# Two score tiles instead of one during the first batch, first query tails by SP's queue, and separate first-batch priorities, in a list-scheduled attention and mixing kernel

## The chip, the cores and the metric

One core of a Trainium2 chip runs the whole program. The metric is the device time of one execution in microseconds (us); the median of three timed executions before the change is 1014.8 us (1014.17 to 1015.2). The profile comes from one further execution.

## What is computed

The shapes are batch 8, 8 heads, sequence 576, head size 64, model size 512, all fp32. Each batch goes through attention in which scores below the row maximum less `tau` are dropped, and then through a token and channel mixing block. Cut to what matters:

```python
scores = scale * np.matmul(q, k.transpose(0, 1, 3, 2))
thresh = np.max(scores, axis=-1, keepdims=True) - tau
scores = np.where(scores >= thresh, scores, -1000000000.0)
attn = np.exp(scores - np.max(scores, axis=-1, keepdims=True))
attn = attn / (np.sum(attn, axis=-1, keepdims=True) + 1e-09)
x = heads_merged(np.matmul(attn, v))
theta = x @ w_theta
y = einsum('ts,bsd->btd', w_tok_r, x * cos(theta)) + einsum('ts,bsd->btd', w_tok_i, x * sin(theta))
u = x + y
out = u + np.maximum(u @ w_ch, 0.0)
```

## The kernel before

**The work.** The eight heads of a batch are four pairs, and each pair has nine score halves of 128 query rows by 576 keys (two heads by four blocks, and one half that holds the 64 last queries of both heads, the "tails"). For a half, TensorE (PE) writes the scores into a tile `s_ps` of two PSUM banks (line 633); VectorE (DVE) copies them out as `sc` and keeps the row minimum (648); ScalarE (ACT) adds the offset (660) and takes the exponential (669); DVE masks and sums (677, `s_sb`); PE transposes the result in four or five 128x128 pieces into one-bank tiles `t_ps` (717, 753); ACT copies those out (728, 730, 757, 761). When the nine halves of a pair are there, forty matmuls make its output `o_ps` in two banks (801).

Four pairs make a batch, and then its mixing runs (`mixture`): angles `m_ps` (939), sines on ACT, transposes `z_ps` (1053), the token product `y_ps` (1103), and the channel product (939 again). The mixing of one batch runs beside the attention of the next.

**The weights.** `w_theta`, `w_tok` and `w_ch` come in as wider numbers. During the first batch, each of nine token chunks and four `w_theta` chunks is loaded as `wraw`, goes through ACT (334, the absolute value `mag`), five DVE instructions (338, 342, 347, 352, 356), ACT (361, the high part), PE (385, 386, into `w_ps`) and ACT (389, the low part).

**The order.** Nothing is scheduled by the compiler. `Plan` collects every piece of work with its engine, an assumed duration, what it needs, a rank, and the slots it takes from named pots. `Plan.run` then walks an assumed clock: at each step it takes the engine that can start soonest and, among that engine's works that could start within a small slack, the one of the lowest rank; the instructions are written out in that order. Ranks come from the table `LEAD`. On the chip each engine runs its list in order and waits on semaphores.

PSUM has eight banks: the pot `pair` has one slot (two banks, for `s_ps`), the pot `bank` has six (one bank each, for `t_ps`, `w_ps`, `o_ps`, `r_ps`, `m_ps`, `y_ps`, `z_ps`). While the plan's clock is under 190 us, the slot `bank5` is kept for dummy matmuls `fill_ps` (line 274): 14 at the start, and some in every gap on PE that the plan sees above 0.5 us.

For pair 0 the two tail pieces of the queries are loaded by ACT's DMA queue (line 287) ahead of everything else on ACT; all other loads are SP's.

Of the kernel before, what the change touches and what calls it, by code (L numbers as in the profile page):

```python
# [10 lines left out]
F32 = mybir.dt.float32  # L11
# [18 lines left out]
STEP = 3.2  # L30
# [6 lines left out]
FILL = 0.2165  # L37
FILL_GAP = 0.5
# [48 lines left out]
class Plan:  # L87
# [9 lines left out]
    def run(self):  # L97
# [7 lines left out]
        filling = True  # L105
        if self.filler:
            pot, slot, fill = self.filler
            pot.free[slot] = NEVER
            fill(14)
        wait = {e: [w for w in self.works if w.eng == e and not w.left] for e in engines}  # L110
        todo = len(self.works)
        while todo:
# [22 lines left out]
            if self.filler and filling and w.eng == "PE":  # L135
                gap = at - free["PE"]
                if free["PE"] > FILL_UNTIL:
                    filling = False
                    pot.free[slot] = at
                elif free["PE"] > 0.0 and gap > FILL_GAP:  # L140
                    fill(int((gap - 0.2) / FILL))
# [24 lines left out]
def tile_attn_moe(  # L166
# [26 lines left out]

    plan = Plan()
    pots = {}
# [4 lines left out]
    for name, n in (  # L200
# [17 lines left out]
    def lead(name):  # L218
        return LEAD[name] * STEP
# [14 lines left out]
    FIRST = 4.9  # L234
# [33 lines left out]
    spare = []  # L268

    def fill(n):  # L270
        if not spare:
            spare.append(psum.tile([P, 512], F32, tag="bank5", name="fill_ps", bufs=1))
        for _ in range(n):
            nc.tensor.matmul(spare[0], dummy[:, :P], dummy, start=True, stop=True)  # L274

    plan.filler = (pots["bank"], 5, fill)
# [177 lines left out]
    def at(t):  # L454
        return t * STEP

    def first_parts(pr, qr, kr, dq, dk, rank):
# [23 lines left out]
        t = on_act(0.2, tail_high, [plan.add("ACT", 0.0, int, (), -99.0, FIRST - HOP)], rank, (pr.tails,))  # L481
# [8 lines left out]
    def prepare(n):  # L490

        pr = pairs[n] = SimpleNamespace(n=n, b=n // NP, p=n % NP, st=[], values=[], normal=[], a={}, scores=[[], []])
        rank = at(NU * n) + lead("prep")
# [99 lines left out]
    def attention(h):  # L593
# [176 lines left out]
        if k == NU - 1:  # L770
            values(pr, at(h) + lead("values"))
# [475 lines left out]
```

## Time and profile before

| | |
|---|---|
| median of three timed runs | 1014.8 us |
| profiled execution | 1013.25 us, its span 1011.4 us |
| PE busy | 999.1 us, 99% |
| DVE busy | 774.2 us, 77% |
| ACT busy | 647.1 us, 64% |
| GpSimd (POOL) busy | 234.4 us, 23% |
| granted TensorE clock, mean | 0.997 |
| dummy matmuls | 73, busy 24.1 us |

Busy times of PE count an instruction until its modelled end, so that two matmuls that follow each other overlap in them; the distance between two starts tells what one costs. A share over the whole span hides stages: the first 115 us, in which the first batch's attention and the weights run without any mixing, and the rest have different limits.

### The profile page before, as it was taken

What the parts mean: (1) busy time and instruction counts of PE and PEld (TensorE: products, weight loads), DVE (VectorE), ACT (ScalarE), POOL (GpSimd) and SP (SyncE); (2) the same over time, 40 slices, a digit from 0 to 9 for tenths busy, and PEclk for the clock granted to TensorE, in tenths of its full rate; (3) what the DMA queues carried; (4) which work ended last, traced back from release to release, by engine and by line L of the source; (5) the groups of instructions that cost most, each with busy time, mean ns of one, the idle gap of its engine ahead of it and who ended that gap; (6) DMA issues with size and microseconds to landing.
All of it is one profiled execution on the core that took longest, in us unless ns stands there. A gap on an engine that the chain in (4) does not pass through costs nothing.

```text
span 1011.4 us, 20944 instructions
## 1 busy us (share of the span) xinstructions
PE 999.1 (99%) x7597; PEld 896.5 (89%) x7597; DVE 774.2 (77%) x2038; ACT 647.1 (64%) x1292; POOL 234.4 (23%) x162
## 2 busy tenths in 40 slices
PE   7999999999999999999999999999999999999998
PEld 5777789889999999999999989899999999999898
DVE  5999788877987688766987679776888679876563
ACT  4888888645776468654785467764686448854430
POOL 1111123032342114311341123421143113400100
PEclk8999999999999999999999999999999999999999
DMA  6568756657654575337744475445763377441502
GB/s 198 157 191 239 212 147 183 163 166 228 170 128 119 140 215 155 98 96 203 198 126 117 98 227 174 108 119 156 217 160 82 90 204 214 112 101 34 172 22 68
DMA packets 86950, 151.89 MB, mean 150 GB/s; under 512 B 27200, under 2 KB 36672, under 8 KB 86848
## 3 DMA queue, kind: packets, MB, share of 16 engines
q1 hardware_dynamic: 86544, 150.53, 53.8%
q8 instruction: 60, 0.98, 0.4%
q14 instruction: 42, 0.34, 0.1%
q10 hardware_dynamic: 304, 0.03, 0.0%
HBM read 81.89 MB, written 13.78 MB: 95 GB/s over the span
## 4 chain that ended last, share of the span: by engine, by line
PE 95%; DVE 3%; DMA 1%; issue 0%; ACT 0%; POOL 0%; ACTq 0%; POOLq 0%
PE y_ps L1103 23%; PE m_ps L939 20%; PE s_ps L633 16%; PE o_ps L801 16%; PE t_ps L717 12%; PE z_ps L1053 3%; PE t_ps L753 2%; PE w_ps L385 2%; PE fill_ps L274 1%; DMA tail_raw<-in_qT_dram 1%; DVE sc L648 1%; DVE s_sb L677 1%; PE w_ps L386 0%; PE r_ps L832 0%; DVE bits L347 0%
## 5 line engine op out<-in xcount | busy, mean ns | idle before, releaser
L648 DVE TENSOR_SCALAR_CACHE_REDUCE sc<-s_ps,small 128x576 f32<-128x576 f32 x288 | 234.0, 812 | 59.6 <-PE s_ps L633 57.6
L677 DVE SCALAR_TENSOR_TENSOR s_sb<-sc,nm,s_sb 128x576 f32<-128x576 f32 x288 | 237.8, 838 | 23.9 <-ACT s_sb L669 23.1
L669 ACT ACTIVATE s_sb<-sc,nm 128x576 f32<-128x576 f32 x288 | 221.8, 783 | 25.1 <-DVE sc L648 24.8
L728 ACT COPY a<-t_ps 128x512 f32<-128x512 f32 x256 | 148.2, 589 | 100.0 <-PE t_ps L717 99.4
L633 PE MATMUL s_ps<-kd,qq 128*128 128x288 f32 x992 | 181.0, 304 | 0.6 <-DVE sc L648 0.3
L717 PE MATMUL t_ps<-ident,s_sb 128*128 128x128 f32 x1152 | 170.4, 273 | 0.0
L1103 PE MATMUL y_ps<-wt_l,zh 128*128 128x288 f32 x576 | 167.1, 304 | 0.0
L1103 PE MATMUL y_ps<-wt_h,zh 128*128 128x288 f32 x576 | 166.4, 307 | 0.0
L801 PE MATMUL o_ps<-a,v 128*64 128x256 f32 (+1 forms) x1280 | 162.3, 408 | 0.0
L633 PEld LDWEIGHTS s_ps<-kd,qq 128*128 128x128 f32 x992 | 143.6, 189 | 8.0 <-DVE sc L648 5.8
L801 PEld LDWEIGHTS o_ps<-a,v 128*64 128x64 f32 x1280 | 89.1, 137 | 63.9 <-issue 5.3
L717 PEld LDWEIGHTS t_ps<-ident,s_sb 128*128 128x128 f32 x1152 | 137.2, 140 | 6.6 <-issue 5.3
L297 POOL TENSOR_TENSOR khl<-kraw,khl 128x576 fp32r<-128x576 f32 x31 | 48.4, 1562 | 357.2 <-ACT khl L529 195.0
L1103 PEld LDWEIGHTS y_ps<-wt_l,zh 128*128 128x128 f32 x576 | 108.4, 189 | 0.2
L1103 PEld LDWEIGHTS y_ps<-wt_h,zh 128*128 128x128 f32 x576 | 108.0, 189 | 0.5
L1103 PE MATMUL y_ps<-wt_h,zl 128*128 128x288 f32 x576 | 107.2, 298 | 0.0
L1034 POOL TENSOR_TENSOR z<-z,xT 128x576 f32<-128x576 f32 x56 | 80.2, 1465 | 85.6 <-ACT z L1019 85.6
L939 PE MATMUL m_ps<-xh,wm 128*128 128x288 f32 x512 | 94.0, 303 | 0.0
L939 PE MATMUL m_ps<-uh,wm 128*128 128x288 f32 x512 | 92.1, 303 | 0.6 <-DVE xT L1157 0.6
L812 ACT COPY xT<-o_ps 128x320 f32<-128x320 f32 x64 | 25.6, 400 | 100.7 <-PE o_ps L801 100.7
L1103 PEld LDWEIGHTS y_ps<-wt_h,zl 128*128 128x128 f32 x576 | 85.7, 188 | 0.0
L939 PEld LDWEIGHTS m_ps<-uh,wm 128*128 128x128 f32 x512 | 74.4, 189 | 3.4 <-issue 2.3
(98 smaller groups left out, 1433.2 us busy)
## 6 DMA issues: line engine op xcount, KB each, us to landing
wm<-wm_dram SPq DMA_DIRECT2D x64, 512.0 KB
kd<-khl SPq DMA_DIRECT2D x62, 288.0 KB
qq<-qhl SPq DMA_DIRECT2D x124, 128.0 KB
kd<-khl SPq DMA_DIRECT2D x62, 256.0 KB
v<-in_vp_dram SPq DMA_DIRECT2D x32, 320.0 KB
kraw<-in_kT_dram SPq DMA_DIRECT2D x32, 288.0 KB
qraw<-in_qT_dram SPq DMA_DIRECT2D x32, 288.0 KB
rb<-rows_dram SPq DMA_DIRECT2D x64, 144.0 KB
```

Source lines behind the costliest of these rows:

```text
L297: eng.tensor_tensor(out=out, in0=a, in1=b, op=ALU.subtract)
L633: nc.tensor.matmul(ps.tile[:, half, to], st, kk[:, fr], start=(x == 0), stop=(x == len(terms) - 1))
L648: nc.vector.tensor_scalar(out=sc.tile.rearrange("p (a b) -> p a b", a=2), in0=ps.tile[:, :, :HS], scalar1=gate, scalar2=None, op0=ALU.mult ...
L669: nc.scalar.activation(out=u.s.tile[:, j], in_=sc.tile, func=AF.Exp, bias=nm.tile[:, 0:1], scale=-1.0)
L677: nc.vector.scalar_tensor_tensor(out=e, in0=sc.tile, scalar=nm.tile[:, 1:2], in1=e, op0=ALU.is_le, op1=ALU.mult, accum_out=pr.rows.tile[:, ...
L717: nc.tensor.transpose(out=bank.tile[:, c * P : (c + 1) * P], in_=sf[:, k0 + c * P : k0 + (c + 1) * P], identity=ident)
L728: nc.scalar.copy(out=t.a[:, :, j, q0 : q0 + P], in_=bank.tile.rearrange("p (c q) -> p c q", c=4))
L801: nc.tensor.matmul(bank.tile[64 * j : 64 * j + 64, :w], st, mv, start=(c == 0), stop=(c == 4))
L939: nc.tensor.matmul(banks[h].tile[:, :HS], wm.tile[:, a, c, :], x[:, h * HS : (h + 1) * HS], start=(key == 0), stop=(key == 11),)
L1034: eng.tensor_tensor(out=zi, in0=zi, in1=xs[m].x.tile, op=ALU.mult)
L1053: nc.tensor.transpose(out=bank.tile[:, i * P : (i + 1) * P], in_=z.tile[:, c : c + P], identity=ident)
L1103: nc.tensor.matmul(bank.tile[:, :HS], st, (wt_l if wl else wt_h)[:, c, hs], start=(k + q == 0), stop=(k + q == 26),)
```

## The change

The PSUM pool is split. A second slot of the pot `pair` and the slots `bank4` and `bank5` share the same two banks in time. At first a pool `psum0` holds the second `pair` slot, so scores have two tiles of two banks, and the other tiles have four banks. When the plan's clock has passed `split` (114.84) and that slot is free, the pool is closed, a pool `psum1` is opened in its place, the `pair` slot is taken out for good, and the two new `bank` slots come in: one pair and six banks from then on, as before.

The dummy matmuls lose their own bank: they take any `bank` slot that is free early enough, 12 or more of them before the first real matmul (how many follows from the plan), and then in gaps above 0.4 us where a slot is free.

The two tail pieces of pair 0's queries are loaded by SP, behind the first `kraw`, and their copy on ACT gets a rank of its own place in the plan. Most entries of `LEAD` get a second value that is added in the first batch only; the weights' ranks change (`wt`, `wt_step`, and new `wk`, `wk_step`). The first token product no longer waits for all token chunks. The assumed duration of the score copy goes from 0.68 to 0.74, with its `pair` slot free 0.08 before the plan's end of it. No computing instruction is added or removed but the dummies.

```diff
-FILL = 0.2165
-FILL_GAP = 0.5
+FILL = 0.228
+FILL_GAP = 0.4
...
-    wt=1.24, wt_step=-3.72, wch=0.63, wch_step=-5.29, wlow=10.19, xh=-17.5, xlast=15.0, angle=1.82, ztok=1.52,
+    wt=0.48, wt_step=-10.83, wch=-3.05, wch_step=-0.24, wlow=14.42, xh=-17.5, xlast=15.0, angle=1.82, ztok=1.52,
...
-    cev=-16.07, dma=1.13, hop=0.13,
+    cev=-16.07, dma=1.13, hop=0.13, split=114.84, wk=-17.47, wk_step=-2.88, score0=-31.88, empty0=-6.42,
+    offset0=15.77, power0=16.19, mask0=-7.4, flip0=-2.74, evict0=-0.54, flip50=-11.41, values0=-13.64,
+    vevict0=-110.27, norm0=-7.09, prep0=-17.86, vload0=10.11, inv0=21.92, times0=17.78, mix0=-2.15, span0=0.08,
...
-        filling = True
-        if self.filler:
-            pot, slot, fill = self.filler
-            pot.free[slot] = NEVER
-            fill(14)
+        filled = False
+        pair, bank = self.pots["pair"], self.pots["bank"]
+        bank.free[4] = bank.free[5] = NEVER
+        split = False
...
+            if not split and at > LEAD["split"] and pair.free[1] < NEVER:
+                split = True
+                bank.free[4] = bank.free[5] = max(at, pair.free[1])
+                pair.free[1] = NEVER
+                self.resplit()
+            if w.eng == "PE" and free["PE"] < FILL_UNTIL:
                 gap = at - free["PE"]
...
+                slot = min(range(4), key=lambda k: bank.free[k])
+                if not filled:
+                    filled = True
+                    self.filler(12 + max(0, int((at - 6.7) / FILL)), slot)
+                elif gap > FILL_GAP and bank.free[slot] < free["PE"] - 0.5:
+                    self.filler(int((gap - 0.2) / FILL), slot)
+                    bank.free[slot] = at
...
-        ("pair", 1), ("bank", 6), ("raw", 3), ("wm", 3), ("z", 3), ("xh", 4), ("xl", 4), ("zh4", 4), ("zl4", 4),
+        ("pair", 2), ("bank", 6), ("raw", 3), ("wm", 3), ("z", 3), ("xh", 4), ("xl", 4), ("zh4", 4), ("zl4", 4),
...
+        if (tag, h.slot) in (("pair", 1), ("bank", 4), ("bank", 5)):
+            p = extra[-1]
...
-    for j in range(2):
-        r = slice(64 * j, 64 * j + 64)
-        nc.scalar.dma_start(tail_raw[r, r], qT[0, 0, j, :, 512:])
...
-        t = on_act(0.2, tail_high, [plan.add("ACT", 0.0, int, (), -99.0, FIRST - HOP)], rank, (pr.tails,))
+        def load_tail(r):
+            return lambda: nc.sync.dma_start(tail_raw[r, r], qT[0, 0, r.start // 64, :, 512:])
+
+        loads = []
+        for j in range(2):
+            w = on_sp(load_tail(slice(64 * j, 64 * j + 64)), loads[-1:] and [issued(loads[-1])], rank - 0.05, (), 16)
+            w.ready = 1.45
+            loads.append(w)
+        t = on_act(0.2, tail_high, loads, rank, (pr.tails,))
...
-        d1 = on_dve(0.68, empty, [s], at(h) + lead("empty"), (sc, nm), 0.08)
-        ps.until(d1)
+        d1 = on_dve(0.74, empty, [s], at(h) + lead("empty", n // NP), (sc, nm), 0.08)
+        ps.until((d1, -0.08))
...
-                    if b == 0 and m == 0:
-                        need += [w for r in wt_ready for w in r]
```

How the order moves is seen in three places. The first is the start of ACT's list. `tails` is the copy of the tail pieces, `mag` the first step of a weight chunk, `part` the high half of the first keys or queries. Before:

```order
L258 DMA small<-in_tau_dram 128x1
L287 DMA tail_raw<-in_qT_dram 64x64 x2
L288 ACT_TABLE_LOAD
L476 CAST tails<-tail_raw 128x128
L334 ACTIVATE mag<-wraw 128x576 x2
L361 ACTIVATE wt_h<-bits 128x576
L464 CAST part<-kraw 128x576
L464 CAST part<-qraw 128x576
```

Now:

```order
L275 DMA small<-in_tau_dram 128x1
L302 ACT_TABLE_LOAD
L348 ACTIVATE mag<-wraw 128x576 x2
L375 ACTIVATE wt_h<-bits 128x576
L478 CAST part<-kraw 128x576
L490 CAST tails<-tail_raw 128x128
L478 CAST part<-qraw 128x576
```

The two tail loads have left ACT's queue, and the copy of the tails stands behind two steps of weights and the keys' high half instead of at the head.

The second place is SP's list at the start, with the loads of the first weight chunks, keys, queries and values. Before:

```order
L329 DMA wraw<-in_w_tok_dram 128x1152 x2
L507 DMA kraw<-in_kT_dram 128x576
L507 DMA qraw<-in_qT_dram 128x576
L516 DMA v<-in_vp_dram 128x640
L507 DMA kraw<-in_kT_dram 128x576
```

Now:

```order
L343 DMA wraw<-in_w_tok_dram 128x1152 x2
L529 DMA kraw<-in_kT_dram 128x576
L496 DMA tail_raw<-in_qT_dram 64x64 x2
L529 DMA qraw<-in_qT_dram 128x576
L529 DMA kraw<-in_kT_dram 128x576
```

The tail loads stand behind the first keys and ahead of the first queries; the weight chunks keep the head.

The third place is PE's list in pair 0, from the second chunk's last sum on. A half's scores are six matmuls of 288 columns, or nine in three widths. Before:

```order
L386 MATMUL w_ps<-wt_h,minus 128x288
L633 MATMUL s_ps<-part 128x64 x3
L633 MATMUL s_ps<-part 128x224 x3
L633 MATMUL s_ps<-part 128x288 x3
L717 MATMUL t_ps<-ident,s_sb 128x128 x4
L274 MATMUL fill_ps<-dummy 128x512 x2
L717 MATMUL t_ps<-ident,s_sb 128x128 x4
L633 MATMUL s_ps<-part 128x288 x6
L274 MATMUL fill_ps<-dummy 128x512 x4
L753 MATMUL t_ps<-ident,s_sb 128x128
```

Now:

```order
L400 MATMUL w_ps<-wt_h,minus 128x288
L655 MATMUL s_ps<-part 128x64 x3
L655 MATMUL s_ps<-part 128x224 x3
L655 MATMUL s_ps<-part 128x288 x9
L739 MATMUL t_ps<-ident,s_sb 128x128 x4
L655 MATMUL s_ps<-part 128x64 x3
L655 MATMUL s_ps<-part 128x224 x3
L655 MATMUL s_ps<-part 128x288 x9
L775 MATMUL t_ps<-ident,s_sb 128x128
```

Two halves' scores now follow each other (the nine rows of 288 columns are three of one half and six of the next), and the dummies between them are gone. In the whole list 50 dummies stand in place of 73: 31 at the head in place of 14, and 19 later in place of 59. Ahead of the first angle matmul `m_ps` stand 214 score matmuls, where there were 198.

## Rows read from the trace of the kernel before

**Rows 1.** The chain that ended last, in order of time: products o_ps.

```profile
115.47 5.00 PE o_ps L801 x40
...
266.52 5.00 PE o_ps L801 x40
...
853.46 5.00 PE o_ps L801 x40
```

**Rows 2.** Busy time of each engine by stretch: start:end, us, engines, PEclk, DMA.

```profile
10.00:115.00 105.00, 101.84 (x622) 76.46 (x623) 99.26 (x228) 89.56 (x209) 16.23 (x10) 0.97 0.68 192
115.00:145.00 30.00, 30.00 (x227) 26.27 (x225) 24.12 (x64) 21.84 (x51) 5.60 (x4) 1.00 0.71 197
...
266.00:384.00 118.00, 118.00 (x930) 108.03 (x931) 91.51 (x253) 76.13 (x148) 31.61 (x21) 1.00 0.55 150
```

**Rows 3.** The same of the dummies alone: PE and weight loads.

```profile
10.00:115.00 105.00, 17.24 (x54) 9.43 (x54) 0.97 0.68 192
115.00:145.00 30.00, 1.56 (x5) 0.81 (x5) 1.00 0.71 197
```

**Rows 4.** Groups by line, 10 to 115: busy, mean ns, idle before.

```profile
L677 DVE SCALAR_TENSOR_TENSOR s_sb<-sc,nm,s_sb 128x576 f32<-128x576 f32 x37 | 31.7, 862 | 1.1 <-ACT s_sb L669 1.1
L648 DVE TENSOR_SCALAR_CACHE_REDUCE sc<-s_ps,small 128x576 f32<-128x576 f32 x38 | 30.8, 811 | 2.7 <-PE s_ps L633 2.6
...
L728 ACT COPY a<-t_ps 128x512 f32<-128x512 f32 x32 | 18.3, 587 | 1.1 <-PE t_ps L717 0.9
```

**Rows 5.** Waits, 10 to 115: total us, times, longest.

```profile
PEld s_ps L633 <- DVE sc L648: 6.6, 21, 0.5
...
DVE mag L338 <- ACT mag L334: 1.5, 3, 1.0
```

**Rows 6.** Instructions in time, ACT then DVE, 9 to 11.

```profile
9.04 0.30 ACT L476 CAST tails<-tail_raw 128x128 fp32r<-128x128 f32 x1 [5.07 <-DMA tail_raw<-in_qT_dram]
9.25 1.33 ACT L334 ACTIVATE mag<-wraw 128x576 f32<-128x576 f32 x2
...
10.00 0.46 DVE L338 TENSOR_SCALAR mag<-mag 128x576 f32<-128x576 f32 x1 [0.28 <-ACT mag L334]
```

**Rows 7.** GB/s moved, 0 to 25, in 40 equal slices; SP's sixth issue.

```profile
GB/s 0 0 59 81 170 258 148 192 251 361 394 384 388 415 402 405 315 167 16 0 0 0 0 0 81 206 391 413 406 413 361 258 221 207 184 133 141 98 0 53
...
6.60 0.33 SPq L507 DMA_DIRECT2D kraw<-in_kT_dram  x1
```

**Rows 8.** Instructions in time on PE: first dummies, first real matmul, later dummies.

```profile
1.45 5.32 PE L274 MATMUL fill_ps<-dummy 128*128 128x512 f32 x14 [1.45 <-DVE dummy L243]
11.89 1.30 PE L385 MATMUL w_ps<-bits,ident 128*128 128x288 f32 x2 [5.12 <-DVE bits L347]
...
16.33 1.09 PE L274 MATMUL fill_ps<-dummy 128*128 128x512 f32 x4
```

**Rows 9.** Busy time and granted clock in short stretches, columns as in Rows 2.

```profile
7.00:12.00 5.00, 0.11 (x1) 0.14 (x1) 2.20 (x6) 1.75 (x4) 0.00 (x0) 0.68 0.80 304
12.00:16.00 4.00, 3.86 (x12) 2.75 (x13) 4.00 (x8) 2.98 (x7) 0.00 (x0) 0.54 0.16 24
```

**Rows 10.** Instructions in time, POOL and DVE, 43 to 49.

```profile
43.59 1.58 POOL L297 TENSOR_TENSOR khl<-kraw,khl 128x576 fp32r<-128x576 f32 x1 [20.46 <-ACT khl L529]
...
43.81 1.97 DVE L677 SCALAR_TENSOR_TENSOR s_sb<-sc,nm,s_sb 128x576 f32<-128x576 f32 x1
...
47.98 0.80 DVE L677 SCALAR_TENSOR_TENSOR s_sb<-sc,nm,s_sb 128x576 f32<-128x576 f32 x1
48.72 0.07 DVE L677 DVE_READ_ACCUMULATOR s_sb<-sc,nm,s_sb 128x1 f32 x1
```

**Rows 11.** Instructions in time on PE, one half at 51.

```profile
50.92 0.69 PE L633 MATMUL s_ps<-kd,qq 128*128 128x288 f32 x4
51.45 0.60 PE L717 MATMUL t_ps<-ident,s_sb 128*128 128x128 f32 x4
51.89 0.27 PE L753 MATMUL t_ps<-ident,s_sb 128*128 128x128 f32 x1
```

More of the change, by code (lines that the diff above doesn't have):

```diff
@@ L192, in tile_attn_moe, with resplit @@
     psum = ctx.enter_context(tc.tile_pool(name="psum", bufs=1, space=PSUM))
+    first = tc.tile_pool(name="psum0", bufs=1, space=PSUM)
+    extra = [first.__enter__()]
+    def resplit():
+        first.__exit__(None, None, None)
+        extra.append(ctx.enter_context(tc.tile_pool(name="psum1", bufs=1, space=PSUM)))
     plan = Plan()
+    plan.resplit = resplit
     pots = {}
@@ L266, in tile_attn_moe, with fill @@
     nc.vector.tensor_tensor(out=span, in0=tau_sb, in1=span, op=ALU.add)
[L268 to L272, printed above, removed]
+    def fill(n, slot):
+        h = hold("bank")
+        h.slot = slot
+        t = get(h, [P, 512], F32, "fill_ps")
         for _ in range(n):
-            nc.tensor.matmul(spare[0], dummy[:, :P], dummy, start=True, stop=True)
-    plan.filler = (pots["bank"], 5, fill)
+            nc.tensor.matmul(t, dummy[:, :P], dummy, start=True, stop=True)
+    plan.filler = fill
+    plan.pots = pots
     wt_h = const.tile([P, NK, S], F32R, name="wt_h")
@@ L642, in attention @@
             need, passes = pr.q_in[j] + pr.k_in[j], 4
-        s = score_pe[h] = on_pe(passes, score, need, at(h) + lead("score"), (ps,))
+        s = score_pe[h] = on_pe(passes, score, need, at(h) + lead("score", n // NP), (ps,))
         def empty():
@@ L730, in evict @@
                 nc.scalar.copy(out=t.a[:, :, :, :64], in_=bank.tile.rearrange("p (c j q) -> p c j q", c=4, j=2))
-        f = on_pe(4, flip, [d3] + t.flips[:1], at(h) + lead("flip"), (bank, t.h) if first else (bank,), TURN_PACE, 0.2)
+        f = on_pe(4, flip, [d3] + t.flips[:1], at(h) + lead("flip", n // NP), (bank, t.h) if first else (bank,), TURN_PACE, 0.2)
         u.flips.append(f)
         t.flips.append(f)
-        a = on_act(0.48, evict, [f] + t.evicts[:1], at(h) + lead("evict"))
+        a = on_act(0.48, evict, [f] + t.evicts[:1], at(h) + lead("evict", n // NP))
         bank.until(a)
@@ L746, in twice @@
                     nc.scalar.copy(out=sf[:, S:SP], in_=sf[:, 512:S])
-                need = [on_act(0.14, twice, [d3], at(h) + lead("mask"))]
+                need = [on_act(0.14, twice, [d3], at(h) + lead("mask", n // NP))]
             def flip5():
@@ L861, in times @@
             nc.vector.tensor_tensor(out=x, in0=x, in1=rb.tile, op=ALU.mult)
-        v = on_dve(0.33, invert, pr.st, rank + lead("inv"), (), 0.085, True)
+        v = on_dve(0.33, invert, pr.st, rank + lead("inv", pr.b), (), 0.085, True)
         f = on_pe(1, turn, [v], rank, (bank,), TURN_PACE, 0.2)
-        a = on_act(0.15, take, [f], rank + lead("inv"), (turned,))
+        a = on_act(0.15, take, [f], rank + lead("inv", pr.b), (turned,))
         pr.rows.until(f)
@@ L869, in normalize @@
         for j in range(3):
-            w.append(on_sp(write(j), [a] + [issued(x) for x in w[-1:]], rank + lead("inv"), (flat,) if j == 0 else (), 2))
+            w.append(on_sp(write(j), [a] + [issued(x) for x in w[-1:]], rank + lead("inv", pr.b), (flat,) if j == 0 else (), 2))
         turned.until(*w)
@@ L873, in normalize @@
         for j in range(2):
-            r.append(on_sp(read(j), w + [issued(x) for x in r], rank + lead("inv"), (rb,) if j == 0 else (), 144))
+            r.append(on_sp(read(j), w + [issued(x) for x in r], rank + lead("inv", pr.b), (rb,) if j == 0 else (), 144))
         flat.until(*r)
-        n1 = on_dve(0.675, times, r + pr.normal, rank + lead("times"), (), 0.085, True)
+        n1 = on_dve(0.675, times, r + pr.normal, rank + lead("times", pr.b), (), 0.085, True)
         rb.until(n1)
@@ L885, in mixture @@
         xs = [pairs[b * NP + c] for c in range(NM)]
-        start = at(NU * NP * (b + 1)) + lead("mix")
+        start = at(NU * NP * (b + 1)) + lead("mix", b)
         total = 96 * PACE * (LEAD["angle"] + LEAD["chan"]) + 36 * TURN_PACE * LEAD["ztr"] + 216 * PACE * LEAD["ztok"]
-        span_ = at(NU * NP) * LEAD["span"]
+        span_ = at(NU * NP) * (LEAD["span"] + (0.0 if b else LEAD["span0"]))
         spent = [0.0]
```

40 lines of the change are left out of this document (15 added, 25 removed).

## The prediction

> **What bounds the kernel now.** I read the chain that ended last first. The product `o_ps` of a batch's second pair ends one lap at 266.52 and stands at 853.46 five batches later [rows 1]: 586.94 / 5 = 117.4 us a batch. In such a batch PE is busy for the whole stretch, while DVE has 91.51 of 118 us [rows 2]. The reader should see a pace that PE alone sets; no dummy is left there (73 in all, 54 + 5 of them from 10 to 145 [rows 3], the first 14 ahead of that). The change leaves PE's work there as it is, so a gain or loss has to arise before about 145 us and is then carried, unshrunk, to the end.
>
> The busy table by stretch shows what is different early. From 10 to 115, DVE is busy 99.26 of 105 us [rows 2]; PE's 101.84 us hold 17.24 us of dummies [rows 3] and overlap besides. So DVE ends that stage: it carries 36 halves and 13 weight chunks at once. That the batch's last product starts at 115.47 [rows 1] is DVE's doing; a microsecond cut from DVE's start or waits there brings it a microsecond nearer.
>
> DVE's wall of 105 us has two parts that are not work of its own. It is idle 105 - 99.26 = 5.74 us, of it 2.7 us ahead of score copies that wait for the scores, 1.1 us ahead of masks [rows 4], 1.5 us ahead of `mag` that ACT has not made yet [rows 5]. And some instructions are stretched: a mask took 1.97 us beside a POOL subtraction of 1.58 us that began 0.22 us earlier, another 0.80 us with POOL quiet [rows 10]. The change leaves POOL's work in place, so I leave the stretch in.
>
> **The start: -2.65 us.** ACT waits 5.07 us for the tail pieces, copies them at 9.04, and only then, at 9.25, begins `mag`; DVE's first weight step starts at 10.00, 0.75 us behind ACT's [rows 6]. In the changed order `mag` is at ACT's head. When could it start? The first chunk is 576 KB and heads SP's queue; the first nine slices of 0.625 us moved (59 + 81 + 170 + 258 + 148 + 192 + 251) x 0.625 = 724 KB by 5.6 us, and 590 KB (576 x 1.024) by about 5.1 us. SP's next key load, the first that had to wait for an earlier load's end, was let go at 6.60 [rows 7]. I take 6.60 for the landing. ACT begins `mag` then in place of 9.25, DVE follows 0.75 us later, at 7.35 in place of 10.00: 2.65 us. The ends: 5.1 would give 4.15 us, and a chunk that lands only just before 9.25 gives nothing. Not below nothing: tails and queries go one or two places back, but ACT's next steps in front of them are two `mag` and two casts, 0.65 us apart each, which take until about 9.3 anyway.
>
> The seventeen more dummies at the head cost at most 1.09 / 4 = 0.27 us each [rows 8], 4.6 us, so they run from 6.77 to about 11.4, a gap in which PE now waits 5.12 us for DVE. The first weight sum can end only with DVE's fifth step, which with the start moved stands near 10.6. That could hold PE 0.8 us, but DVE's own list is full at that point; I put it at nothing, with 0.8 us as its other end. A side gain goes with it: after the 5.12 us without work the granted clock was 0.68 from 7 to 12 and 0.54 from 12 to 16, which is mostly the level of 1.2 GHz, while DVE was busy 4.00 of 4 us [rows 9]. PE's faster sums there are hidden by DVE: nothing.
>
> **The second score tile: -3.4 us.** With one tile, a half's scores can start only when DVE has copied the half before. PE's weight loads wait for that 21 times, 6.6 us in all [rows 5], and the copy after it then waits for PE: the 2.7 us. With two tiles the next scores are written while DVE masks; PE's list in pair 0 shows it, two halves' scores in a row. I take the 2.7 us as won and a quarter of the other 2.8 us of `mag` and mask waits, which the new ranks move but do not remove: 2.7 + 0.7 = 3.4 us. The ends are 0 (the waits come back elsewhere) and 5.74 us, all idle time. PE has room for it: the dummies' 17.24 us and 3.16 us of idle time.
>
> **Four banks for the rest: +0.5 us.** Pieces, weight sums and products share four banks until the split. A bank is held while PE writes it and ACT copies it, 0.587 us [rows 4], and a product holds two for 5.00 us. A wait of PE for ACT costs the end only where DVE then runs dry. The near end is 0; the far end is one copy of 0.587 us, twice, behind each of four products and on the path, 4.7 us less the part that PE's room hides. I take 0.5 us, near the low end, because today's waits of PE are short (6.6 us over 21).
>
> **The rest: nothing.** The split waits for a score tile that is free by then. The tail loads are two issues on SP of small size. Removing the wait of the first token product for all chunks matters only if chunks were late then; PE has no gap at that point. Ranks of later batches stay.
>
> **Sum.** -2.65 - 3.4 + 0.5 = -5.55 us on the profiled execution's 1013.25, so 1007.7; the median lies 1.55 us above that execution, so I forecast **1009.3 us** as the median. A measurement of this kernel can tell about 0.2%, 2.0 us, from no change.
>
> **Rivals.**
>
> *Only the start is won, and the mixing begins later.* By the order, 214 score matmuls stand ahead of the first angle product, not 198: four halves of four. A half costs DVE 2 x 0.74 us (mask 47.98 to 48.72 [rows 10], the score copy alike) and PE 0.53 + 0.44 us (50.92 to 51.89 [rows 11]), so four more such halves without mixing leave PE 4 x (1.48 - 0.97) = 2.0 us short. If the waits come back elsewhere too, that is -2.65 + 2.0: 1014.1 us. For it: DVE is nearly full. Against it: the same four halves are then missing later, where PE is the bound.
>
> *Both ends of the gain.* The chunk lands at 5.1 and all of DVE's idle time goes: -4.15 - 5.74 = -9.9, 1004.9 us. For it: 40 fewer dummies after the head, each of which stood in a gap that the plan saw.
>
> *The banks become the bound (slower).* From 10 to 115 some 74 bank uses stand on PE's list: 36 four-piece transposes, 16 single ones, 22 weight sums. If PE waits one ACT copy, 0.587 us, at k of them, its room of 17.24 + 3.16 = 20.4 us and the start's 2.65 us are used up at k = 39, and it is slower by over 2.0 us from k = 43. At 44 waits plus the 2.0 us of the first rival: 25.8 - 20.4 - 2.65 + 2.0 = +4.8, 1019.6 us. Against it: ACT's idle time ahead of these copies is there because it waits for PE (1.1 us [rows 4]), not the other way round. The Trainium skill (Perfetto Trace Analysis, section Matmuls) says that independent groups of matmuls should rotate through different PSUM banks so that the copying out of one overlaps the next; by that rule six banks to four is a loss for the pieces and one tile to two a gain for the scores. The rows bear out the second half, and nothing in them yet shows the first.
>
> *The clock falls.* With 19 dummies in place of 59 after the head, PE may stand long enough to drop to 1.2 GHz once. Rows 9 price it: 5 x 0.32 + 4 x 0.46 = 3.4 us of lost full-speed time, so 1009.3 + 3.4 = 1012.7 us. For it: it fell after a gap of 5.12 us [rows 8]. Against it: from 16 us on it is full, and no gap of that size is left in so full a stage. The Trainium skill (TensorE: Matmul & The Clock Gate, section What's actually happening) has the throttled clock as the default that activity lifts; by that rule fewer dummies is a risk, and the trace agrees so far as its one drop follows its one long gap.
>
> **How the numbers follow.** Forecast 0.57, only the start 0.14, both ends 0.18, banks 0.07, clock 0.04. Faster by over 0.2% (under 1012.8): all of the forecast and of both ends, half of the clock, a third of the first rival that wins a little more: 0.57 + 0.18 + 0.02 + 0.05 = 0.82. Slower: the banks, 0.07. The same: the remaining 0.11. The range reaches from a little under both ends, 1004.0, to a little over the first rival, 1014.5; what it leaves out is the banks and the far part of both ends, under 2 in 10.
>
> **What would show it.** `mag` first on ACT near 6.6 and DVE's first step near 7.4; no stretch at 1.2 GHz after the head; DVE idle ahead of score copies under 1 us up to the fourth product; that product near 110 in place of 115.47; 117.4 us a batch as before. It is wrong if DVE's first step stays after 9, if PE's weight loads or matmuls for `t_ps`, `w_ps` or `o_ps` wait for ACT by several us, or if the fourth product is early and the eighth is not.

## The result and the profile after

The changed kernel takes 1005.49 us (median of 4 runs, 1004.23 to 1005.69), the kernel before 1014.95 us (4 runs beside it, 1014.17 to 1015.2): a ratio of 0.9905 with a 95% interval of 0.9888 to 0.9923, 9.46 us less. The forecast was 1009.3 us: the direction was right and the time lies in the range, near its lower end, but the gain came out at 9.5 where 5.6 stood. The profiled executions differ by 7.7 us (1005.51 against 1013.25; spans 1003.4 and 1011.4). The profiled one of before lies 1.7 us under its median and that of the change at its median, so 1.7 of the 9.46 us is spread between executions, which the traces can't place.

The chain that ended last, in order of time (start, us, engine, tile and line), answers to [rows 1]:

```profile
108.35 5.00 PE o_ps L823 x40
...
257.03 5.00 PE o_ps L823 x40
...
845.16 5.00 PE o_ps L823 x40
```

The first batch's fourth product, its last, starts 7.12 us earlier than in [rows 1]. The ninth (the third batch's first; the prediction calls it a second pair's) starts 9.49 us earlier, and the same one five batches on 8.30 us. A batch takes (845.16 - 257.03) / 5 = 117.6 us where it took 117.4. So the gain is made before 257 us, and 1.2 us of it is given back over five batches. Of this 0.6 us falls in one lap, 492.02 to 610.15, which takes 118.1 us (117.6 before): the chain holds a load of queries there that the chain of before doesn't have, and PE stands 0.5 us.

```profile
600.11 4.83 DMA qraw<-in_qT_dram
610.15 5.00 PE o_ps L823 x40
```

Busy time by stretch, columns as in [rows 2] and [rows 9]:

```profile
10.00:115.00 105.00, 99.14 (x655) 74.52 (x655) 101.52 (x244) 93.36 (x224) 18.16 (x11) 1.00 0.74 210
115.00:145.00 30.00, 29.91 (x228) 26.31 (x227) 23.92 (x58) 23.30 (x52) 9.35 (x7) 1.00 0.67 182
...
7.00:12.00 5.00, 5.00 (x26) 4.17 (x24) 4.89 (x10) 3.73 (x7) 0.00 (x0) 1.00 0.76 286
12.00:16.00 4.00, 3.98 (x23) 3.06 (x22) 3.71 (x9) 2.33 (x6) 3.09 (x1) 1.00 0.90 314
```

DVE is idle 105 - 101.52 = 3.48 us of the stage where it was idle 5.74, and the clock is full from 7 us on. Instructions in time at the start, PE, ACT and DVE, answer to [rows 6, 8]:

```profile
1.45 8.76 PE L290 MATMUL fill_ps<-dummy 128*128 128x512 f32 x31 [1.45 <-DVE dummy L260]
6.23 0.72 ACT L348 ACTIVATE mag<-wraw 128x576 f32<-128x576 f32 x1 [3.79 <-DMA wraw<-in_w_tok_dram]
6.98 0.46 DVE L352 TENSOR_SCALAR mag<-mag 128x576 f32<-128x576 f32 x1 [1.03 <-ACT mag L348]
9.92 0.29 ACT L490 CAST tails<-tail_raw 128x128 fp32r<-128x128 f32 x1
10.05 0.65 PE L399 MATMUL w_ps<-bits,ident 128*128 128x288 f32 x2
```

The waits from 10 to 115 us (total us, times, longest) answer to [rows 5]; the score copy's wait for PE there was 2.6 us by [rows 4]:

```profile
PEld s_ps L655 <- DVE sc L670: 5.5, 18, 0.6
...
DVE s_sb L699 <- ACT s_sb L691: 1.4, 2, 1.1
...
DVE sc L670 <- PE s_ps L655: 0.7, 2, 0.6
```

Where the 9.49 us came from can be counted in two pieces, cut at the fourth product. The first is DVE's stage, from its first weight step to that product. Before it ran from 10.00 [rows 6] to 115.47 [rows 1], after it from 6.98 to 108.35. Busy time in these stretches, before and then after:

```profile
10.00:115.47 105.47, 102.31 (x626) 76.77 (x628) 99.62 (x229) 90.03 (x210) 16.23 (x10) 0.97 0.68 192
```

```profile
6.98:108.35 101.37, 95.52 (x616) 72.60 (x616) 98.10 (x233) 89.05 (x212) 17.06 (x10) 1.00 0.75 209
```

DVE starts 3.02 us earlier, is idle 5.85 - 3.27 = 2.58 us less, and works 99.62 - 98.10 = 1.52 us less: 7.12 us, all of it. The last of the three is not for want of work: two more score copies are made there (40, not 38; 1.1 us more), and one subtraction of 0.8 us, `xl`, has moved behind the cut. What changed is how long some of the weights' steps took. By line from 10 to 115.47 before and from 6.98 to 108.35 after:

```profile
L356 DVE SCALAR_TENSOR_TENSOR w<-wraw,mag 128x576 fp32r<-128x576 uint32 (+1 forms) x13 | 11.4, 876 | 0.0
L347 DVE SCALAR_TENSOR_TENSOR bits<-wraw,bits 128x576 uint32<-128x576 uint32 (+1 forms) x13 | 10.6, 817 | 0.1
L352 DVE TENSOR_SCALAR mag<-bits 128x576 uint32<-128x576 uint32 (+1 forms) x13 | 6.3, 481 | 0.1
...
L297 DVE TENSOR_TENSOR xl<-xT,xh 128x576 fp32r<-128x576 f32 x1 | 0.8, 755 | 0.0
```

```profile
L370 DVE SCALAR_TENSOR_TENSOR w<-wraw,mag 128x576 fp32r<-128x576 uint32 (+1 forms) x13 | 10.0, 766 | 0.0
L361 DVE SCALAR_TENSOR_TENSOR bits<-wraw,bits 128x576 uint32<-128x576 uint32 (+1 forms) x13 | 9.4, 724 | 0.1
L366 DVE TENSOR_SCALAR mag<-bits 128x576 uint32<-128x576 uint32 (+1 forms) x13 | 7.0, 537 | 0.1
```

The first two give 1.4 + 1.2 = 2.6 us, with the same mix of widths in both kernels, and the third takes 0.7 us back. The means moved by single steps: of the 13 `bits` at L347 the longest took 1.78 us, of those at L361 0.76 us, while the middle ones took 0.75 us in both; of `mag` the longest took 0.93 us at L352 and 1.64 us at L366. POOL runs ten subtractions in either stretch, and each of these long steps ran beside one, as in [rows 10]. The longest of all, before:

```profile
99.83 1.68 POOL L297 TENSOR_TENSOR qhl<-qraw,qhl 128x576 fp32r<-128x576 f32 x1 [1.96 <-ACT qhl L525]
...
100.16 1.90 DVE L356 SCALAR_TENSOR_TENSOR w<-wraw,mag 128x512 fp32r<-128x512 uint32 x1
```

The second piece is PE's, from the fourth product to the ninth: 151.05 us before, 148.68 after, 2.37 less. Score matmuls alone (PE, weight loads, then DVE's copies of the scores), before and then after, up to the fourth product and from there to the ninth:

```profile
7.00:115.47 108.47, 34.98 (x194) 26.95 (x194) 31.14 (x76) 0.97 0.69 198
115.47:266.52 151.05, 35.48 (x198) 28.57 (x198) 39.34 (x96) 1.00 0.66 183
```

```profile
6.98:108.35 101.37, 34.64 (x206) 27.58 (x206) 32.16 (x80) 1.00 0.75 209
108.35:257.03 148.68, 33.19 (x186) 26.88 (x186) 37.75 (x92) 1.00 0.68 190
```

Twelve score matmuls, three halves of four, have gone from the stretch that PE bounds to the one that DVE bounds. Transposes, weight sums, products and mixing matmuls have the same counts on either side of the cut in both kernels. At 0.53 / 4 us each [rows 11] the twelve are 1.6 us, by estimate; the dummies in the same stretch fell from 1.56 to 0.63 us. Together 2.5 us, against 2.37 measured. This is a count and not a test; the tests follow.

### The profile page after: what moved, and what is told of

It is laid out like the page before. It is cut to its first block, busy times and chain, and to the rows that moved or that the text cites. A ratio compares the mean times of both kernels' runs of the same rounds, so it can differ in the third digit from the quotient of the medians.

```text
span 1003.4 us, 20961 instructions
## 1 busy us (share of the span) xinstructions
PE 990.8 (99%) x7574; PEld 890.5 (89%) x7574; DVE 770.6 (77%) x2038; ACT 647.3 (65%) x1292; POOL 234.7 (23%) x162
## 4 chain that ended last, share of the span: by engine, by line
PE 91%; DVE 5%; issue 2%; DMA 1%; ACT 1%; SPq 0%; DVEq 0%; ACTq 0%
PE y_ps L1123 23%; PE m_ps L961 19%; PE o_ps L823 15%; PE s_ps L655 15%; PE t_ps L739 12%; PE z_ps L1075 3%; PE t_ps L775 2%; DVE s_sb L699 2%; DVE sc L670 1%; PE w_ps L399 1%; PE fill_ps L290 1%; DMA qraw<-in_qT_dram 0%; ACT a L750 0%; DMA wm<-wm_dram 0%; PE r_ps L854 0%
## 5 line engine op out<-in xcount | busy, mean ns | idle before, releaser
L699 DVE SCALAR_TENSOR_TENSOR s_sb<-sc,nm,s_sb 128x576 f32<-128x576 f32 x288 | 241.7, 850 | 20.2 <-ACT s_sb L691 19.3
L750 ACT COPY a<-t_ps 128x512 f32<-128x512 f32 x256 | 150.3, 590 | 100.5 <-PE t_ps L739 99.3
L739 PE MATMUL t_ps<-ident,s_sb 128*128 128x128 f32 x1152 | 173.3, 274 | 1.3 <-DVE s_sb L699 0.6
L961 PE MATMUL m_ps<-xh,wm 128*128 128x288 f32 x512 | 97.4, 307 | 0.0
L961 PEld LDWEIGHTS m_ps<-xh,wm 128*128 128x128 f32 x512 | 75.5, 189 | 2.8 <-issue 2.7
```

The lines of the kernel that those rows point to most:

```text
L699: nc.vector.scalar_tensor_tensor(out=e, in0=sc.tile, scalar=nm.tile[:, 1:2], in1=e, op0=ALU.is_le, op1=ALU.mult, accum_out=pr.rows.tile[:, ...
L739: nc.tensor.transpose(out=bank.tile[:, c * P : (c + 1) * P], in_=sf[:, k0 + c * P : k0 + (c + 1) * P], identity=ident)
L750: nc.scalar.copy(out=t.a[:, :, j, q0 : q0 + P], in_=bank.tile.rearrange("p (c q) -> p c q", c=4))
L961: nc.tensor.matmul(banks[h].tile[:, :HS], wm.tile[:, a, c, :], x[:, h * HS : (h + 1) * HS], start=(key == 0), stop=(key == 11),)
```

## The experiments

Two kinds of kernel were run. Some keep the changed order word for word and alter one thing, so their prices hold no new order. The others change a buffer or a rank before the plan is made, so the whole first batch is ordered anew, and the price holds the order that came out too. Times of before are 1014.4 to 1014.6 us beside them. Dummies compute nothing of the output, so no run leaves any of it out.

The mean granted clock of an execution goes into the prices too. The change's four executions all have 1.00. In several of the runs it differs from one execution to the next, and the one with the lowest clock then took longest: 1007.95 us at 0.996 without dummies after the head, 1017.54 at 0.997 with the split at 60, 1020.54 at 0.993 with all old ranks.

### The same order, one thing altered

**Tails back in front of ACT.** The two loads go back to ACT's queue and the copy to ACT's head; their places in the plan stay, empty.

```diff
+    for j in range(2):
+        r = slice(64 * j, 64 * j + 64)
+        nc.scalar.dma_start(tail_raw[r, r], qT[0, 0, j, :, 512:])
...
+    nc.scalar.copy(out=tails[:, 0], in_=tail_raw)
...
-            nc.scalar.copy(out=tails[:, 0], in_=tail_raw)
+            return None
...
-            return lambda: nc.sync.dma_start(tail_raw[r, r], qT[0, 0, r.start // 64, :, 512:])
+            return lambda: None
```

> The changed kernel in its own order, but the two tail loads on ACT's queue and their copy at ACT's head again, as before the change. Theory 'start' (the microseconds that DVE begins earlier are carried to the end): DVE's first weight step near 10.0 in place of 6.98, 3.0 us slower than the changed kernel's 1005.49, so 1008.5 us. Rival 'slack' (with two score tiles DVE makes the late start good later): at most 1 us slower, under 1006.5.

Measured 1007.82 us (1007.7 to 1009.59), 2.3 us over the change. DVE, in time:

```profile
10.38 0.46 DVE L356 TENSOR_SCALAR mag<-mag 128x576 f32<-128x576 f32 x1 [3.32 <-ACT mag L352]
```

The start is 10.38 - 6.98 = 3.40 us later, the fourth product 111.74 - 108.35 = 3.39 us, and the end 2.3 us. The start carries through to the fourth product whole, and about two thirds of it to the end. The time lies between the two theories, nearer to the start's; the 95% intervals of the ratios to before, 0.9923 to 0.9956 here and 0.9888 to 0.9923 for the change, just touch.

**Fourteen dummies at the head.**

```diff
-                    self.filler(12 + max(0, int((at - 6.7) / FILL)), slot)
+                    self.filler(14, slot)
```

> The changed kernel in its own order with 14 dummies at the head in place of 31. Rival 'clock' (a good part of the gain is that TensorE never falls to 1.2 GHz at the head): the granted clock falls again for some 7 us, 2 us slower or more, 1007.5. My theory (PE's slow stretch lies beside DVE, which ends the stage): within 0.5 us, 1005.5 to 1006.

Measured 1006.29 us (1005.71 to 1006.65), 0.8 us over the change. Busy time by stretch:

```profile
7.00:12.00 5.00, 3.02 (x10) 1.65 (x10) 4.77 (x9) 3.81 (x8) 0.00 (x0) 0.90 0.79 297
12.00:16.00 4.00, 4.00 (x19) 3.37 (x18) 3.51 (x8) 1.91 (x4) 3.20 (x1) 0.70 0.89 311
```

PE now stands twice ahead of the first weight's sums, and once more at 53 us:

```profile
9.02 0.72 PE L399 MATMUL w_ps<-bits,ident 128*128 128x288 f32 x2 [1.26 <-DVE bits L361]
10.46 0.40 PE L399 MATMUL w_ps<-w,ident_r 128*128 128x288 f32 x1 [0.71 <-DVE w L370]
...
55.07 1.05 PE L655 MATMUL s_ps<-kd,qq 128*128 128x288 f32 x4 [1.94 <-issue]
```

```profile
55.40:58.80 3.40, 3.40 (x12) 2.83 (x11) 3.37 (x8) 3.40 (x9) 0.00 (x0) 0.50 0.65 194
```

Behind the head the granted clock is 0.90 and then 0.70, and from 55.4 to 58.8 us it is 0.50, so parts of the stage ran at 1.2 GHz although the later dummies are all there. DVE has 0.12 + 0.20 us less work done by 16 us, and its score copies wait 1.9 us for PE in the stage, where they waited 0.7. The longer head is worth under a microsecond, more than my theory's half and less than the rival's 2, and the intervals of the two ratios overlap. How much of it is the second fall isn't shown.

**No dummies after the head.**

```diff
-                    self.filler(int((gap - 0.2) / FILL), slot)
```

> The changed kernel in its own order without the 19 dummies that follow the head. Rival 'clock': without them the granted clock falls in some gap and it is 2 us slower or more, over 1007.5. My theory (no gap is long enough, and PE waits where the dummies stood): within 0.5 us of 1005.5, and the clock full.

Measured 1005.57 us (1004.78 to 1007.95), the changed kernel's time. Busy time by stretch:

```profile
10.00:115.00 105.00, 95.90 (x639) 72.13 (x638) 101.49 (x244) 93.28 (x223) 17.48 (x11) 1.00 0.75 210
115.00:145.00 30.00, 29.58 (x226) 25.93 (x225) 23.95 (x57) 23.35 (x52) 9.51 (x7) 1.00 0.66 182
```

PE's busy time falls by 3.2 us in the first stretch, DVE's by 0.03, and the clock stays full in this execution. In the median the later dummies buy nothing that shows. But only three of the four executions have a mean granted clock of 0.999 or more (1004.78 to 1006.14 us); the fourth has 0.996 and took 1007.95, and where its clock fell isn't on record. Whether the later dummies keep such falls away is open: with them there are four executions, all at 1.00.

### Tiles and banks, ordered anew

**The tails on SP, and nothing else of the change.** Built on the kernel before.

```diff
-    for j in range(2):
-        r = slice(64 * j, 64 * j + 64)
-        nc.scalar.dma_start(tail_raw[r, r], qT[0, 0, j, :, 512:])
...
-        t = on_act(0.2, tail_high, [plan.add("ACT", 0.0, int, (), -99.0, FIRST - HOP)], rank, (pr.tails,))
+        def load_tail(r):
+            return lambda: nc.sync.dma_start(tail_raw[r, r], qT[0, 0, r.start // 64, :, 512:])
...
+            w = on_sp(load_tail(slice(64 * j, 64 * j + 64)), loads[-1:] and [issued(loads[-1])], rank - 0.05, (), 16)
+            w.ready = 1.45
+            loads.append(w)
+        t = on_act(0.2, tail_high, loads, rank, (pr.tails,))
```

> The kernel before with one change: the tail loads on SP and their copy in the plan. The plan is made anew, its priorities stay the old ones. Theory 'start': about 3.0 us faster than before's 1014.95, so 1012. Rival (an earlier start helps only together with the second tile): within 1 us of before, 1014 to 1015.

Measured 1017.58 us (1017.18 to 1018.23), a ratio to before of 1.003 (1.0018 to 1.0042): slower, which neither theory had. DVE's first step starts at 7.21 us, 2.79 earlier than in [rows 6], but the fourth product at 118.41, 2.9 later than in [rows 1]. DVE's waits, 10 to 115 us:

```profile
DVE sc L653 <- PE s_ps L638: 7.3, 12, 1.4
DVE mag L335 <- ACT mag L331: 1.6, 2, 1.0
```

The early start was won and then lost, most of it to waits at the one score tile, 7.3 us where [rows 4] have 2.6.

**One score tile and six banks** in the changed kernel.

```diff
-        ("pair", 2), ("bank", 6), ("raw", 3), ("wm", 3), ("z", 3), ("xh", 4), ("xl", 4), ("zh4", 4), ("zl4", 4),
+        ("pair", 1), ("bank", 6), ("raw", 3), ("wm", 3), ("z", 3), ("xh", 4), ("xl", 4), ("zh4", 4), ("zl4", 4),
...
-        bank.free[4] = bank.free[5] = NEVER
-        split = False
+        split = True
```

> The changed kernel with one score tile and six banks from the start, as before the change; tails on SP, dummies and priorities as changed, the plan made anew. Theory 'tile' (the second tile gives what is left of the 9.5 us beside the start's 3.0): about 6 us slower than the changed kernel, 1011.5. Rival 'priorities' (the new first-batch priorities and not the tile do it): within 2 us, 1005.5 to 1007.5.

Measured 1021.21 us (1019.47 to 1022.13), 15.7 us over the change and slower than before (1.0064, 1.0049 to 1.0079), which is beyond both theories.

**One score tile and four banks up to the split**, the two others unused till then.

```diff
+            if not split and at > LEAD["split"]:
...
+                bank.free[4] = bank.free[5] = at
-                pair.free[1] = NEVER
-                self.resplit()
...
-        ("pair", 2), ("bank", 6), ("raw", 3), ("wm", 3), ("z", 3), ("xh", 4), ("xl", 4), ("zh4", 4), ("zl4", 4),
+        ("pair", 1), ("bank", 6), ("raw", 3), ("wm", 3), ("z", 3), ("xh", 4), ("xl", 4), ("zh4", 4), ("zl4", 4),
```

> As e4 (one score tile, changed priorities), but the rest has four banks until the split, as in the changed kernel, so two banks lie unused. Against e4's 1021.2 us: if four banks cost nothing, within 1 us of it, 1020 to 1022. Rival 'banks' (the forecast's term of 0.5 us up to 4.7 us): 1023 us or more.

Measured 1018.77 us (1017.94 to 1020.47). With two banks fewer it is 2.4 us faster than with six, and its fourth product starts at 117.85 in place of 120.06. DVE's waits for scores in the stage are 4.3 us (5.5 with six banks). The comparison isn't clean, since the two orders differ and the granted clock from 10 to 115 us is 0.98 with six banks and 1.00 with four; but up to the split, four banks cost nothing that these runs show. Taking the second tile out, with the changed ranks left around it, costs 1018.77 - 1005.49 = 13.3 us, far more than all the idle time of DVE that [rows 2] leave to win. So that is the price of a tile in a set of ranks made for two, not of the tile alone.

**The split at 150** in place of 114.84.

```diff
-    cev=-16.07, dma=1.13, hop=0.13, split=114.84, wk=-17.47, wk_step=-2.88, score0=-31.88, empty0=-6.42,
+    cev=-16.07, dma=1.13, hop=0.13, split=150.0, wk=-17.47, wk_step=-2.88, score0=-31.88, empty0=-6.42,
```

> The changed kernel with the split at 150 on the plan's clock. In the changed kernel DVE waits 4.2 us for scores from 115 to 205. Theory 'tile': with two tiles for longer some of it goes, 1003 to 1005 us. Rival 'banks': the mixing's products need the six banks from 115 on, 1007 us or more.

Measured 1011.89 us (1010.61 to 1013.6), 6.4 us over the change. Busy time by stretch:

```profile
10.00:115.00 105.00, 98.65 (x656) 74.60 (x655) 101.51 (x244) 93.24 (x223) 17.58 (x11) 1.00 0.75 210
115.00:145.00 30.00, 26.37 (x187) 23.70 (x184) 26.12 (x65) 21.87 (x49) 8.33 (x6) 1.00 0.63 173
```

Up to 115 us it does what the changed kernel does (101.51 us of DVE against 101.52). Then PE runs 187 instructions where the changed kernel runs 228, and the fifth product, the second batch's first, starts at 147.45 in place of 132.91. PE's longest waits from 115 to 150 us, and the clock at their end:

```profile
PE z_ps L1075 <- DVE th L311: 1.6, 1, 1.6
PE z_ps L1075 <- DVE zl L311: 1.3, 1, 1.3
```

```profile
145.00:150.00 5.00, 4.50 (x22) 2.87 (x24) 3.17 (x7) 2.57 (x6) 2.32 (x3) 0.66 1.02 252
```

Both DVE steps read a bank empty (`m_ps`, `z_ps`), so they fit a want of banks: four are enough for the scores' stage and too few once the mixing runs beside it. But they are 2.9 of the 6.4 us, PE's weight load ahead of the first waited 1.8 us for POOL's `z`, and the rest holds the order made anew and the fall of the clock. So the banks are the likely cause and not a shown one.

The Trainium skill (Perfetto Trace Analysis, section Matmuls) asks that independent matmul groups rotate through different PSUM banks. No run here shows a loss by two banks fewer up to the split; behind it this run agrees with the rule as far as its two waits go.

**The split at 60.**

```diff
-    cev=-16.07, dma=1.13, hop=0.13, split=114.84, wk=-17.47, wk_step=-2.88, score0=-31.88, empty0=-6.42,
+    cev=-16.07, dma=1.13, hop=0.13, split=60.0, wk=-17.47, wk_step=-2.88, score0=-31.88, empty0=-6.42,
```

> The changed kernel with the split at 60 in place of 114.84 on the plan's clock, the plan made anew. Theory 'tile': the second tile is taken away for the later half of the stage and DVE waits for scores there again; about half of what one tile costs (e4 lies 15.7 us above), 1010 to 1014 us. Rival 'banks' (six banks are worth more than the second tile once pair 0 is through): 1005.5 us or less.

Measured 1012.88 us (1011.69 to 1017.54), 7.4 us over the change. The fourth product is as early as in the changed kernel (108.30 against 108.35), though DVE waits 4.0 us for scores. The loss is behind it: DVE stands 5.99 us ahead of an angle step at 139.99, and the first mixed output starts at 154.0 us where the changed kernel has 144.7. Less is also done ahead of its fourth product, 194 score matmuls where the changed kernel has 206:

```profile
7.00:108.30 101.30, 33.03 (x194) 25.88 (x194) 30.79 (x77) 1.00 0.78 211
```

So the fourth product alone doesn't tell the time. Whether the tile is wanted to the stage's end, or the ranks only fit the split that they were made with, this run doesn't tell apart.

### Ranks, ordered anew

**All old ranks, two tiles.** `LEAD` and the weights' loop as before, the rest as changed.

```diff
-    wt=0.48, wt_step=-10.83, wch=-3.05, wch_step=-0.24, wlow=14.42, xh=-17.5, xlast=15.0, angle=1.82, ztok=1.52,
+    wt=1.24, wt_step=-3.72, wch=0.63, wch_step=-5.29, wlow=10.19, xh=-17.5, xlast=15.0, angle=1.82, ztok=1.52,
...
+    split=114.84, score0=0.0, empty0=0.0, offset0=0.0, power0=0.0, mask0=0.0, flip0=0.0, evict0=0.0, flip50=0.0, values0=0.0, vevict0=0.0, norm0=0.0, prep0=0.0, vload0=0.0, inv0=0.0, times0=0.0, mix0=0.0, span0=0.0,
```

> The changed kernel with the priorities of before (no first-batch terms, old ranks of the weights), two score tiles until the split, tails on SP, dummies as changed; the plan made anew. Theory 'tile': DVE waits for scores under 1.5 us from 10 to 115, and most of the gain is there without the priorities: 1007 to 1010 us. Rival 'priorities': without them the tile is worth little, 1013 us or more.

Measured 1015.91 us (1011.53 to 1020.54, 10 runs), a ratio to before of 1.0011 (0.9992 to 1.003): no gain, 10.4 us over the change. DVE waits 3.2 us for scores from 10 to 115 us, not under 1.5. Yet its fourth product starts at 108.12, earlier still than the changed kernel's. Its waits from 115 to 145 us, and the first angle product on PE:

```profile
DVE sc L669 <- PE s_ps L654: 6.3, 4, 3.6
DVE th L1002 <- issue: 6.2, 1, 6.2
...
PE m_ps L960 <- DMA wm<-wm_dram: 1.9, 1, 1.9
```

```profile
130.58 0.50 PE L960 MATMUL m_ps<-xh,wm 128*128 128x288 f32 x2 [1.87 <-DMA wm<-wm_dram]
```

The mixing begins at 130.58 us, 13.8 later than in the changed kernel (116.8). What two tiles seem to win by the fourth product is lost behind it. And part of it was never won, for less is done ahead of that product: 194 score matmuls and 84 for the weights' sums, where the changed kernel has 206 and 88.

```profile
7.00:108.10 101.10, 32.57 (x194) 26.01 (x194) 30.23 (x75) 1.00 0.71 203
```

**Old ranks, but the weights' new ones.** As the run above, with these in `LEAD` and the changed loop:

```diff
+    wt=0.48, wt_step=-10.83, wk=-17.47, wk_step=-2.88, wch=0.63, wch_step=-5.29, wlow=10.19, xh=-17.5, xlast=15.0, angle=1.82, ztok=1.52,
```

> As e5 (two tiles, old priorities, 1015.9 us), with the changed ranks of the weights (wt, wt_step, wk, wk_step) put in and nothing else. Theory 'weights' (two tiles bring the attention forward, and it pays once the w_theta chunks are ready for the mixing): first angle matmul before 120 in place of 130, and 1007 to 1011 us. Rival 'first-batch terms' (the terms of the other works are needed): 1013 us or more.

Measured 1019.98 us (1016.43 to 1022.47, 10 runs), slower than before. The weights' ranks alone don't mend it: the mixing begins at 124.9 us, but DVE now waits 10.2 us for scores before 115 us, and the fourth product is back at 115.44. Part of that is the clock:

```profile
16.00:21.50 5.50, 5.50 (x41) 4.46 (x40) 4.25 (x12) 5.06 (x15) 1.42 (x1) 1.00 0.94 234
21.56:31.80 10.24, 10.24 (x32) 7.98 (x32) 8.65 (x21) 4.67 (x9) 0.00 (x0) 0.50 0.68 175
```

None of its ten executions has a mean above 0.998, and one of those took the least, 1016.43 us. That is still far from 1007 to 1011, so the theory that the weights' ranks carry the gain falls.

**The changed kernel with the weights' old ranks.**

```diff
-    wt=0.48, wt_step=-10.83, wch=-3.05, wch_step=-0.24, wlow=14.42, xh=-17.5, xlast=15.0, angle=1.82, ztok=1.52,
+    wt=1.24, wt_step=-3.72, wch=-3.05, wch_step=-0.24, wlow=14.42, xh=-17.5, xlast=15.0, angle=1.82, ztok=1.52,
...
-        weight_mid(0, w_theta, c, lead("wt") + lead("wt_step") * c)
+        weight_mid(0, w_theta, c, rank)
+        rank += lead("wt_step")
```

> The changed kernel with the old ranks of the weights and everything else as changed. Theory 'weights': the last w_theta sum after 104, the first angle matmul later than the changed kernel's 115.8 by 4 us or more, 1009 to 1014 us. Rival 'first-batch terms': within 1.5 us of the changed kernel, up to 1007 us.

Measured 1025.68 us (1023.97 to 1027.57), the slowest of all, beyond every number expected. The angle product starts at 125.3 us (the changed kernel's at 116.8, not at 115.8 as expected above) and the first mixed output at 185.1, 40.4 us later than in the changed kernel. So in this set the weights' ranks carry 20 us, and put alone into the run above they gained nothing.

**The kernel before with the weights' new ranks.**

```diff
-    wt=1.24, wt_step=-3.72, wch=0.63, wch_step=-5.29, wlow=10.19, xh=-17.5, xlast=15.0, angle=1.82, ztok=1.52,
+    wt=0.48, wt_step=-10.83, wk=-17.47, wk_step=-2.88, wch=0.63, wch_step=-5.29, wlow=10.19, xh=-17.5, xlast=15.0, angle=1.82, ztok=1.52,
...
-        weight_tok(c, rank)
-        rank += lead("wt_step")
+        weight_tok(c, lead("wk") + lead("wk_step") * c)
```

> The kernel before with the changed ranks of the weights alone: one tile, tails on ACT. Theory 'weights and tile are needed together': DVE goes on waiting 2.5 us or more for scores, first angle matmul at 120 or later, within 3 us of before's 1014.6. Rival (the ranks alone give the gain): under 1010 us.

Measured 1021.7 us (1020.86 to 1023.84), 7 us slower than before, which neither theory had: DVE waits 7.0 us for scores at its one tile before 115 us, and the first mixed output starts at 161.8, although the angle product starts at 117.8, earlier than expected.

No run beats the changed kernel; the one without later dummies equals it. Two things stay open. What the second tile is worth in an order that doesn't assume it was not tried, since every order here comes from a plan that knows its tiles. And the lifted wait of the first token product for all chunks was not tried by itself.

## Why the prediction was right, and where its size was off

- **The bound, and where a gain must arise: right.** The 9.49 us stand at 257.03, and PE's pace hardly moves: 117.6 us a batch. "Carried, unshrunk, to the end" failed in part: 8.0 us are left at the end. Of the 1.2 us lost by 845 us, 0.6 go with the late load of queries; what costs the rest wasn't tried. (The product at 266.52 is the third batch's first, not a second pair's; the pace read from it holds.)
- **"The start: -2.65 us": right, a little small.** `mag` begins at 6.23, not 6.60, and DVE at 6.98: 3.02 us. The same-order run shows that a start moved by 3.40 us moves the fourth product by 3.39. It also goes against "unshrunk": about a third of that is lost again before the end. And alone, with one tile and an order made anew, the start gave nothing at all.
- **"Seventeen more dummies at the head: nothing": right within the noise, but not by the end named.** That end was a loss of 0.8 us, PE held by the dummies. PE's first sum is held, from 9.02 in the run with fourteen to 10.05, and it costs nothing that shows. What shows is a gain, 0.8 us by the medians, from PE's faster sums, which the prediction called hidden by DVE.
- **"The second score tile: -3.4 us": borne out, smaller, and not by the tile alone.** The waits for scores fell from 2.6 us [rows 4] to 0.7 as forecast (under 1 us), the mask waits stayed (1.1 us, then 1.4), and all idle time fell by 2.58 us. But with two tiles among the old ranks these waits are 3.2 us, and 10.2, in part by the clock, with the weights' new ranks: the tile allows the overlap, and the order has to use it.
- **"I leave the stretch in": a failed step.** It was set to nothing because POOL's work stays in place. POOL does the same ten subtractions, but in another order they meet other steps: 2.6 us less in two kinds of weight steps, 0.7 more in a third, 1.52 net of all. The forecast had no term for that, and that it helped is luck.
- **"The rest: nothing", and the first rival: the other failed step.** I read that four more halves ahead of the mixing would leave PE 2.0 us short. Three of them had gone ahead by the fourth product, into time that PE had spent on dummies, and they were then missing where PE is the bound, just as the rival's own "against it" said. That is the 1.6 us, with 0.9 us of fewer dummies. In the same step stood "PE has no gap at that point", and that holds: from 115 to 145 us PE is busy 30.00 us before and 29.91 after. But the old ranks with two tiles show how a late mixing costs over ten microseconds behind an early fourth product. The ranks were part of the gain, and I had costed them at nothing.
- **"Four banks for the rest: +0.5 us": nothing that shows**, by the two runs with one tile. The rival in which the banks become the bound is refuted for this split; for a later one it is likely, though not all of its 6.4 us are the banks'.
- **The rival of the falling clock did not come about in the changed kernel.** Its granted clock is 1.00 in every stretch above and in all four executions. It is not refuted as a risk: the clock fell inside the stage with the short head (0.50 from 55.4 us), with the weights' new ranks among the old (0.50 from 21.56) and, by the mean of 0.996, in one of four executions without the later dummies. The Trainium skill (TensorE: Matmul & The Clock Gate, section What's actually happening) has the throttled clock as the default that activity lifts. The traces agree for the start: in the changed kernel the first dummies take 0.63 us each, and from 4.6 us on 0.39.
- **Sum.** 3.02 + 2.58 + 1.52 + 2.37 = 9.49 by 257 us, less 1.2 over the batches and 0.3 at the end: 8.0 us of span, where 5.55 were forecast. The median then differs by 9.46 because the step "the median lies 1.55 us above that execution" doesn't hold for the changed kernel: its median is its profiled execution's time. "Both ends of the gain" gave nearly the right time (1004.9), but by luck, from sums that weren't so: the first weights came at 6.23, not 5.1, and DVE keeps 3.3 us of idle time in the stage. The counted pieces are not all tested: the start is, in the same order; the tile, the ranks and the moved halves only together.

## What to carry to other kernels

Where a list scheduler orders the work, a buffer and the ranks chosen with it have one joint price: here no part that was tried alone gained, taking one out of the set cost from nothing (the later dummies) and 2.3 us (the start) to 20 us (the weights' ranks), and the set gave 9.5. Price single terms with the order held fixed, and ask of a new order which work has moved out of the stretch that the pace-setting engine bounds; count the instructions by tile on both sides of a cut. An early end of the stage in front is worth only as much as the next stage's inputs are ready by then. And look at the granted clock of each execution before a microsecond is put down to an order.

## What was not expected of the hardware

- The same 13 weight steps of DVE took 817 and 876 ns on average in one order and 724 and 766 ns in another, at equal shapes and with the same ten subtractions on POOL. Single steps did it: 1.78 and 1.90 us beside a POOL subtraction, where 0.75 is usual. That POOL is the cause was not tried by itself.
- A POOL subtraction of the usual 1.42 us took 3.09 us at 12.06 in the changed kernel, in a stretch in which DMA engines were busy 0.90 of the time and DVE 3.71 of 4 us. Which of the two stretched it was not tried.
- A wait of PE in front does not by itself tell when the granted clock falls. Without the later dummies PE stood up to 1.2 us at a time and the profiled execution kept 1.00. With the short head 1.94 us without work stand ahead of a fall to 0.50. And in the run with the weights' new ranks among the old, the fall at 21.56 us stands behind 5.5 us in which PE is busy throughout.
